# Strassen's seven block products for two of three output token tiles, on one Trainium2 core

## Chip, cores and metric

The kernel runs on one core of a Trainium2 chip. The metric is the device time of one execution in microseconds, as the median of the runs.

## The reference

Grouped-query attention (8 batches, 16 query heads, 4 key heads, 384 tokens, head size 64) is followed by a gated projection block with a spatial gate over the tokens:

```python
k = np.repeat(k, group, axis=1); v = np.repeat(v, group, axis=1)
scores = scale * np.matmul(q, k.transpose(0, 1, 3, 2))
attn = softmax(scores)                       # over the last axis
x = np.matmul(attn, v).transpose(0, 2, 1, 3).reshape(B, S, H * D)   # 8 x 384 x 1024
h = np.maximum(x @ w_in, 0.0)                # 1024 -> 1024
u, v = h[..., :512], h[..., 512:]
v_n = (v - mean(v)) / np.sqrt(var(v) + 1e-06)
v_s = np.einsum('ts,bsd->btd', w_spatial, v_n) + b_spatial[None, :, None]
out = (u * v_s) @ w_out                      # 512 -> 1024, float32
```

The last line is the output projection that the change is about: for each batch 384 x 512 times 512 x 1024.

## The kernel before

Everything is in float16 on TensorE (PE), with float32 sums in PSUM's eight banks. The 384 tokens of a batch are three tiles of 128. One batch of attention is 18 units (three query tiles, two head pairs, three key tiles); a unit's scores are two matmuls of 512 columns (`units`, L281), whose exponentials ACT writes as `aT` (L293). `weigh` (L301) multiplies them with V in twelve short matmuls, and DVE divides by the sum: a reciprocal (L315) and a product (L317) into `x16`. `x_send` (L341) has SP's queue transpose `x16` into `xt`.

The second half of the work is a stream of pieces, written as a generator, `gated` (L513), batch by batch:

- `v_part(b, st)`: eight matmuls of 512 columns (L357); DVE takes the relu out of PSUM into `vr` (L371). `measure` adds DVE's statistics (L383, L384) at the next `weigh`, or at once in the last batch.
- `u_part(b, m)`: eight matmuls of 384 columns (L438); ACT takes the relu (L449).
- `root` and `norm`: ACT makes the inverse root, DVE `nmr` (L396), and POOL writes the three normalized tiles `vn` (L401).
- `s_part(b, m)`: three matmuls of 384 columns with the spatial weights (L457); DVE adds the bias (`vs`, L469), and POOL multiplies with `uT` into `gT[:, m]` (L474). In the last batch's last m, DVE does the first token tile and POOL the others (L477).
- `o_part(b, tt, half)`: four matmuls of 512 columns, `gT` of 128 tokens against 512 columns of `w_out` (L495), summed in one bank. DVE copies it to `osb` (ACT for the second half of tile 1, L218), and after the second half SP's queue stores the tile (L510).

The output pieces of batch b - 1 are spread over batch b's stream: two after `v_part(b, 0)`, the others before each `s_part(b, m)`; in the last batch one after `v_part(7, 0)`, then one before each `s_part` and one after them. Batch 7's own come at the end.

The main loop (L773) goes in steps of three units. Each step issues six score matmuls, and between these and two groups of `weigh` it pours pieces of the stream in four portions, 0.2, 0.3, 0.1 and 0.4 of a share. The share is a sixth of a batch's planned matmul time:

```python
STEP = (NT * NK * C512 + NM * NK * C384 + NM * NT * C384 + 6 * NM * C512) / SETS
```

(17,496 / 6 = 2,916 ns; 15% less before unit 90). A piece counts at 216 ns for 512 columns and 162 for 384. What was poured too much or too little is carried over. What is left at the end of attention follows without pause. So the queues' order is fixed when the program is written: each engine takes its instructions in it.

PSUM banks are planned at the same time: `bank` (L79) takes the bank with the earliest planned end, and `reads` (L90) moves a planned clock of the reading engine on and sets that end:

```python
def reads(eng, ns, name=None):
    clock[eng] = max(clock[eng], clock[nc.tensor] + 200.0) + ns
    if name:
        done[taken.pop(name)] = clock[eng]
```

Only operations that call `reads` are on this planned clock.

The functions that the diff touches:

Of the kernel before, what the change touches and what calls it, by code (L numbers as in the profile page):

```python
# [9 lines left out]
FP32 = mybir.dt.float32  # L10
FP16 = mybir.dt.float16
I32 = mybir.dt.int32
AF = mybir.ActivationFunctionType
ALU = mybir.AluOpType
# [4 lines left out]
def kernel(  # L19
# [14 lines left out]
    nc = tc.nc  # L34
    P = 128
    B, HQ, S, D = q.shape
    HKV = k.shape[1]
    DM = moe_w_in.shape[0]
    DFF = moe_w_in.shape[1]
    DH = DFF // 2  # L40
    NT = S // P
    NK = DM // P
# [9 lines left out]
    order = ctx.enter_context(ExitStack())  # L52
    order.enter_context(tc.manual_schedule())

    cst = ctx.enter_context(tc.tile_pool(name="cst", bufs=1))
    ld = order.enter_context(tc.tile_pool(name="ld", bufs=2))
    att = order.enter_context(tc.tile_pool(name="att", bufs=2))
    moe = order.enter_context(tc.tile_pool(name="moe", bufs=2))
    small = order.enter_context(tc.tile_pool(name="small", bufs=4))
    ops = order.enter_context(tc.tile_pool(name="ops", bufs=3))  # L60
# [8 lines left out]
            name=nc.get_next_instruction_name(), act_func_set_id=set_id, ins=[], outs=[]  # L69
        )  # L70
    )
    pool, dve, act, sp = nc.gpsimd, nc.vector, nc.scalar, nc.sync
# [6 lines left out]
    def bank(shape, dtype, name):  # L79
        i = min(range(8), key=done.__getitem__)  # L80
        t = ps.tile(shape, dtype, name=name, tag=f"bank{i}")
        clock[nc.tensor] = max(clock[nc.tensor], done[i])
        done[i] = 1e12 + clock[nc.tensor]
        taken[name] = i
        return t

    def spend(ns):
        clock[nc.tensor] += ns
# [6 lines that stand above are left out]
    C512, C384, C128 = 216, 162, 56  # L95
# [59 lines left out]
    w_out16 = cst.tile([P, NM, DM], FP16, name="w_out16")  # L155
# [60 lines left out]
    def copy(eng, o, i, name):  # L216
        reads(eng, 600.0 if name.startswith("po") else 430.0, name)
        (act.copy if eng is act else dve.tensor_copy)(o, i)  # L218
# [45 lines left out]
    aTs, x16s, xts = {}, {}, {}  # L264
# [58 lines left out]
        measure()  # L323

    def new_xt(b):
        xts[b] = att.tile([P, NK, S], FP16, name=f"xt_{b}", tag="xt", bufs=3)

    def x_turn(b, qt, lo, hi, eng):
        if qt == 0 and lo == 0:
# [16 lines left out]
    v_r, v_n, mvs, uTs, gTs = {}, {}, {}, {}, {}  # L346
# [3 lines left out]
    def v_part(b, st, lo=0, hi=NK):  # L350
        if st == 0 and lo == 0:
            mvs[b] = small.tile([P, NT, 2], FP32, name=f"mv_{b}", tag="mv")
        if lo == 0:
            pvs[b, st] = bank([P, 512], FP32, f"pv_{b}_{st}")
        pv = pvs[b, st]
        for kt in range(lo, hi):
            nc.tensor.matmul(  # L357
                pv,
                xts[b][:, kt, st * P : (st + 1) * P],
                w_in16[:, kt, DH:DFF],  # L360
                start=(kt == 0),
                stop=(kt == NK - 1),
            )
            spend(C512)
            if kt < NK - 1:
                yield C512
        if hi < NK:
            return
        reads(dve, 610.0, f"pv_{b}_{st}")
        vr = moe.tile([P, DH], FP32, name=f"vr_{b}_{st}", tag="vr", bufs=6)  # L370
        dve.tensor_scalar(vr, pv, 0.0, None, op0=ALU.max)  # L371
        v_r[b, st] = vr
        unmeasured.append((b, st))
        if b == B - 1:
            measure()
        yield C512

    def measure():
        while unmeasured:
            b, st = unmeasured.pop()  # L380
            reads(dve, 800.0)
            stats = small.tile([P, 6], FP32, name=f"stats_{b}_{st}", tag="stats")
            dve.bn_stats(stats, v_r[b, st])  # L383
            dve.bn_aggr(mvs[b][:, st], stats)  # L384
# [8 lines left out]
    def norm(b):  # L393
        rstd = mvs[b, "rstd"]
        nmr = small.tile([P, NT], FP32, name=f"nmr_{b}", tag="nmr")
        dve.scalar_tensor_tensor(  # L396
            nmr, mvs[b][:, :, 0], -1.0, rstd, op0=ALU.mult, op1=ALU.mult
        )
        for st in range(NT):
            vn = moe.tile([P, DH], FP16, name=f"vn_{b}_{st}", tag="vn", bufs=6)  # L400
            (dve if b == 0 and st == 1 else pool).tensor_scalar(  # L401
                vn,
                v_r.pop((b, st)),
                rstd[:, st : st + 1],
                nmr[:, st : st + 1],
                op0=ALU.mult,
                op1=ALU.add,
            )
            v_n[b, st] = vn
# [67 lines left out]
                eng.tensor_tensor(gT[:, :, t], vs[:, :, t], uT[:, :, t], ALU.mult)  # L477
        yield C384

    osbs = {}  # L480

    def o_part(b, tt, half):
        last = b == B - 1
        if half == 0:
            osbs[b, tt] = ops.tile([P, DM], FP32, name=f"osb_{b}_{tt}", tag="osb")
        osb = osbs[b, tt]
        rows = out[b].rearrange("(p t) d -> p t d", t=NT)

        parts = [(half * 512, 512, act if half and (last or tt == 1) else dve, sp)]
        if last and tt == NT - 1 and half:  # L490
            parts = [(512, 384, dve, sp), (896, 128, act, act)]
        for c0, width, eng, queue in parts:
            po = bank([P, 512], FP32, f"po_{b}_{tt}_{c0}")
            for m in range(NM):
                nc.tensor.matmul(  # L495
                    po[:, 0:width],
                    gTs[b][:, m, tt * P : (tt + 1) * P],
                    w_out16[:, m, c0 : c0 + width],
                    start=(m == 0),
                    stop=(m == NM - 1),  # L500
                )
                spend(C512 * width / 512)
                if m < NM - 1:
                    yield C512 * width / 512
            cols = slice(c0, c0 + width)
            copy(eng, osb[:, cols], po[:, 0:width], f"po_{b}_{tt}_{c0}")
            if last:
                queue.dma_start(rows[:, tt, cols], osb[:, cols])
            elif half:
                sp.dma_start(rows[:, tt, :], osb)  # L510
            yield C512 * width / 512

    def gated():  # L513
        for b in range(B):
            u0 = b * UNITS
            behind = [(b - 1, tt, half) for tt in range(NT) for half in range(2)] if b else []
            if b == 0:
                for st in range(NT):
                    yield ("from", 6 * st + 7)
                    yield from v_part(b, st, 0, 4)  # L520
                    yield ("from", 6 * st + 10)
                    yield from v_part(b, st, 4, 8)
            else:
                yield ("from", u0 + 12)
                yield from v_part(b, 0)
                for _ in range(1 if b == B - 1 else 2):
                    yield from o_part(*behind.pop(0))
                yield ("from", u0 + 18)
                yield from v_part(b, 1)
                yield ("from", u0 + 24)  # L530
                yield from v_part(b, 2)
            for m in range(NM):
                i = 0
                for x in u_part(b, m):
                    yield x
                    i += 1
                    if (m, i) == (1, 6):
                        root(b)
                    if (m, i) == (2, 3):
                        norm(b)  # L540
                    if (b, m, i) == (B - 1, 2, 5):
                        judge()
            for m in range(NM):
                if (b, m) == (B - 1, 2):
                    count()
                if behind:
                    yield from o_part(*behind.pop(0))
                yield from s_part(b, m)
            if behind:
                yield from o_part(*behind.pop(0))  # L550
        for tt in range(NT):
            for half in range(2):
                yield from o_part(B - 1, tt, half)
# [39 lines left out]
    def at(n, f, *args):  # L593
        todo.setdefault(n, []).append((f, args))
# [92 lines left out]
    at(29, load_v, 2)  # L687
    at(31, load_q, 2, 1, sp, (1, 2))
    at(36, cast_v, 2, pool)
    for j, n in ((0, 34), (1, 36)):  # L690
        at(n, cast_q, 2, j, pool, (1, 2))
        at(n + 1, q_send, 2, j, 1, NT)
# [112 lines left out]
    with tc.If(counted != 0x43000000, preferred_fallthrough_block=False), ExitStack() as ctx:  # L805
        again = ctx.enter_context(tc.tile_pool(name="again", bufs=1))
        t = {
            n: again.tile([P, *w], I32 if n == "i32" else FP32, name=f"again_{n}")
            for n, w in (
                ("qg", (G * D,)), ("sc", (G, S)), ("p16", (16,)), ("row", (DH,)), ("kv", (16 * D,)),  # L810
                ("prod", (16 * D,)), ("one", (4,)), ("w", (4 * DM,)), ("f4", (4,)), ("acc", (DM,)),
                ("x", (DM,)), ("i32", (S,)),
            )
        }
# [224 lines left out]
```

## Time and profile before

| | |
|---|---|
| median of 3 runs | 240.33 us (239.26 to 242.33) |
| profiled execution | 239.11 us |
| span of its instructions | 237.1 us |
| PE matmuls busy | 230.1 us (97%), 2313 instructions |
| PE weight loads (PEld) | 123.7 us (52%) |
| DVE / ACT / POOL busy | 144.0 / 169.3 / 102.1 us |
| granted PE clock | 1.00 in every stage |
| output matmuls (L495) | 188 of 512 columns, 4 of 384, 4 of 128 |

The duration of a single matmul in the profile (380 ns for 512 columns) includes its way through the array; successive ones start closer together, so busy sums of PE do not show the rate. In the groups, the columns are: line, engine, operation, tile written and tiles read, shapes, count, then busy time and the mean of one in ns, then the idle time of the engine just before them and what ended it. The chain of waits is followed back from the last instruction; its lines are start, duration, and the engine and line. In the timeline the columns are start, duration, engine, line and operation.

### The profile page before, as it was taken

What the parts mean: (1) busy time and instruction counts of PE and PEld (TensorE: products, weight loads), DVE (VectorE), ACT (ScalarE), POOL (GpSimd) and SP (SyncE); (2) the same over time, 40 slices, a digit from 0 to 9 for tenths busy, and PEclk for the clock granted to TensorE, in tenths of its full rate; (3) what the DMA queues carried; (4) which work ended last, traced back from release to release, by engine and by line L of the source; (5) the groups of instructions that cost most, each with busy time, mean ns of one, the idle gap of its engine ahead of it and who ended that gap; (6) DMA issues with size and microseconds to landing.
All of it is one profiled execution on the core that took longest, in us unless ns stands there. A gap on an engine that the chain in (4) does not pass through costs nothing.

```text
span 237.1 us, 5939 instructions
## 1 busy us (share of the span) xinstructions
PE 230.1 (97%) x2313; PEld 123.7 (52%) x2313; DVE 144.0 (61%) x382; ACT 169.3 (71%) x349; POOL 102.1 (43%) x149
## 2 busy tenths in 40 slices
PE   7899999999999999999999999999999999999992
PEld 6555655545554546554564555554465455545541
DVE  2668774676456764566656576376645577377462
ACT  2899989968997869977797776985697776402211
POOL 3489583651566343274055700575031500550740
PEclk9999999999999999999999999999999999999999
DMA  6999999999999999989979899479902642340256
GB/s 168 282 319 316 272 145 165 199 292 223 308 227 210 244 374 177 243 240 294 181 230 234 235 211 287 85 250 182 254 3 60 114 174 56 46 177 0 91 212 233
DMA packets 67469, 47.48 MB, mean 200 GB/s; under 512 B 48336, under 2 KB 60416, under 8 KB 67440
## 3 DMA queue, kind: packets, MB, share of 16 engines
q1 hardware_dynamic: 62512, 39.86, 69.9%
q0 software_dynamic: 3952, 6.42, 12.0%
q10 hardware_dynamic: 976, 0.82, 1.2%
q8 instruction: 18, 0.29, 0.5%
q14 instruction: 11, 0.09, 0.1%
HBM read 25.95 MB, written 12.58 MB: 163 GB/s over the span
## 4 chain that ended last, share of the span: by engine, by line
PE 86%; DMA 6%; DVE 2%; SPq 1%; POOL 1%; issue 0%; ACTq 0%; ACT 0%
PE pu L438 17%; PE po L495 17%; PE pv L357 17%; PE sc L281 14%; PE av L301 13%; PE psp L457 6%; DMA q<-in_q_dram 4%; DMA qT<-q 2%; SPq L258 1%; PE qps L240 1%; POOL vn L401 1%; PE xps L334 1%; DVE x L317 1%; DVE qT L218 1%; DVE osb L218 1%; POOL q L206 0%
## 5 line engine op out<-in xcount | busy, mean ns | idle before, releaser
L293 ACT ACTIVATE aT<-sc 128x512 f16<-128x512 f32 x288 | 147.4, 621 | 30.9 <-PE sc L281 30.3
L301 PEld LDWEIGHTS <-aT 128*128 128x128 f16 x1152 | 47.0, 97 | 17.1 <-issue 1.9
L357 PE MATMUL pv<-w_in,xt 128*128 128x512 f16 x192 | 51.0, 380 | 0.1
L301 PE MATMUL av<-v,aT 128*128 128x65 f16 x1152 | 50.5, 193 | 0.0
L495 PE MATMUL po<-w_out,gT 128*128 128x512 f16 (+2 forms) x196 | 50.5, 375 | 0.0
L438 PE MATMUL pu<-xt,w_in 128*128 128x384 f16 x256 | 49.9, 327 | 0.0
L401 POOL TENSOR_SCALAR vn<-vr,rstd,nmr 128x512 f16<-128x512 f32 x23 | 17.6, 779 | 67.0 <-DVE nmr L396 45.6
L474 POOL TENSOR_TENSOR gT<-vs,uT 128x384 f16<-128x384 f32 x31 | 32.4, 1057 | 31.0 <-DVE r_all L315 16.9
L317 DVE TENSOR_TENSOR x<-av,r_all 128x256 f16<-128x256 f32 x96 | 40.8, 424 | 3.3
L281 PE MATMUL sc<-qT,kT 64*128 64x512 f16 x288 | 41.5, 380 | 0.5 <-DVE qT L218 0.2
L315 DVE RECIPROCAL r_all<-av 128x4 f32<-128x4 f32 x96 | 17.1, 179 | 40.5 <-PE av L301 40.1
L218 DVE COPY osb<-po 128x512 f32<-128x512 f32 (+1 forms) x39 | 26.6, 683 | 15.9 <-PE po L495 15.9
L438 PEld LDWEIGHTS <-w_in 128*128 128x128 f16 x256 | 22.1, 98 | 17.1 <-issue 5.5
L449 ACT ACTIVATE uT<-pu 128x384 f16<-128x384 f32 x32 | 15.8, 495 | 16.0 <-PE pu L438 15.8
L495 PEld LDWEIGHTS <-gT 128*128 128x128 f16 x196 | 17.3, 97 | 17.3 <-issue 3.2
L357 PEld LDWEIGHTS <-xt 128*128 128x128 f16 x192 | 15.8, 97 | 17.8 <-issue 5.5
L281 PEld LDWEIGHTS <-kT 64*128 64x128 f16 x288 | 10.9, 94 | 23.7 <-issue 12.3
L457 PE MATMUL psp<-wsT,vn 128*128 128x384 f16 x96 | 22.2, 327 | 0.0
L469 DVE TENSOR_TENSOR vs<-psp,bias_bc 128x384 f32<-128x384 f32 x32 | 17.6, 552 | 7.1 <-PE psp L457 6.9
L203 POOL CAST q<-q 128x768 f16<-128x768 f32 x22 | 17.6, 831 | 9.5 <-DMA q<-in_q_dram 4.5
L371 DVE TENSOR_SCALAR vr<-pv 128x512 f32<-128x512 f32 x24 | 16.4, 683 | 8.4 <-PE pv L357 8.3
L383 DVE BATCH_NORM_STATS2 stats<-vr 128x6 f32<-128x512 f32 x24 | 16.4, 685 | 0.1
(55 smaller groups left out, 101.9 us busy)
## 6 DMA issues: line engine op xcount, KB each, us to landing
out_dram<-osb SPq DMA_DIRECT2D x21, 512.0 KB, 3.2
q<-in_q_dram SPq DMA_DIRECT2D x10, 768.0 KB, 5.9
v_None<-in_v_dram SPq DMA_DIRECT2D x6, 384.0 KB, 5.7
w_in<-in_moe_w_in_dram POOLq DMA_DIRECT2D x4, 512.0 KB, 9.8
k_None<-in_k_dram SPq DMA_DIRECT2D x5, 384.0 KB, 3.7
q<-in_q_dram POOLq DMA_DIRECT2D x2, 768.0 KB, 7.6
out_dram<-osb SPq DMA_DIRECT2D x5, 256.0 KB, 3.1
w_out<-in_moe_w_out_dram POOLq DMA_DIRECT2D x2, 512.0 KB, 8.6
```

The source lines that it names most:

```text
L203: eng.tensor_copy(t16[:, :, :, hh, :], src[:, hh])
L218: (act.copy if eng is act else dve.tensor_copy)(o, i)
L281: nc.tensor.matmul(sc, kTs[b][rows, j, kt * P : (kt + 1) * P], qTs[b, j][rows, qt].rearrange("p (r i c) -> p i r c", r=G, i=G), start=True ...
L293: act.activation(a, sc, AF.Exp, scale=scale)
L301: nc.tensor.matmul(av[:, i * (D + 1) : (i + 1) * (D + 1)], aT[:, kt, hh, i * P : (i + 1) * P], v1[b % 2][:, 2 * j + hh, kt, 0 : D + 1], st ...
L317: dve.tensor_tensor(x16s[b][:, qt, c : c + 256].rearrange("p (i d) -> p i d", i=G), o[:, :, 0:D], r.to_broadcast([P, G, D]), ALU.mult,)
L357: nc.tensor.matmul(pv, xts[b][:, kt, st * P : (st + 1) * P], w_in16[:, kt, DH:DFF], start=(kt == 0), stop=(kt == NK - 1),)
L401: (dve if b == 0 and st == 1 else pool).tensor_scalar(vn, v_r.pop((b, st)), rstd[:, st : st + 1], nmr[:, st : st + 1], op0=ALU.mult, op1=A ...
L438: nc.tensor.matmul(pu[:, 0:S], w_in16[:, kt, m * P : (m + 1) * P], xts[b][:, kt, :], start=(kt == 0), stop=(kt == NK - 1),)
L457: nc.tensor.matmul(psp[:, 0:S], v_n[b, st][:, m * P : (m + 1) * P], wsT16[:, st, :], start=(st == 0), stop=(st == NT - 1),)
L474: pool.tensor_tensor(gT, vs, uT, ALU.mult)
L495: nc.tensor.matmul(po[:, 0:width], gTs[b][:, m, tt * P : (tt + 1) * P], w_out16[:, m, c0 : c0 + width], start=(m == 0), stop=(m == NM - 1),)
```

## The change

For batches 1 to 6 (`fast(b)`), token tiles 0 and 1 are taken as one product of two-by-two blocks: A has 128 tokens by 256 inner columns (rows of `gT`), W has 256 inner rows by 512 output columns. Seven products (`f_part(b, n)`, two matmuls each) take the place of eight block products (sixteen matmuls). Their left and right sides are blocks or sums of blocks:

- 1: A11 W11. 2: A12 W21. 3: S4 W22. 4: A22 T4. 5: S1 T1. 6: S2 T2. 7: S3 T3.
- S1 = A21 + A22, S2 = S1 - A11, S3 = A11 - A21, S4 = A12 - S2; they are `gS`, made by `g_combine(b)` on DVE (256 elements a partition each, float16).
- T1 to T4 are sums of blocks of `w_out`, made once by `w_combine` on DVE (1,024 elements a partition, float16) at units 42, 45, 48 and 51.

Product 1 comes at the end of batch b's stream, and ACT copies it to `part`. After `v_part(b + 1, 0)` come `g_combine(b)` and products 2 and 6; products 7 and 5 stand before `s_part(b + 1, 0)`, products 4 and 3 before `s_part(b + 1, 1)`, and tile 2's two pieces before the next two. In batch 7 products 4 and 3 are a place apart, and the last piece follows `s_part(7, 3)`. Each of products 2 to 7 is added on DVE straight from PSUM to a partial sum, product 5 twice. Tile 0 is stored after product 3, tile 1 after product 4. Batches 0 and 7 and all third tiles keep `o_part`. Batch 0's first four output matmul groups keep their places, written in the new form. Buffers of `xt` go from 3 to 2, of `vr` from 6 to 4, of `vn` from 6 to 3.

```diff
-        xts[b] = att.tile([P, NK, S], FP16, name=f"xt_{b}", tag="xt", bufs=3)
+        xts[b] = att.tile([P, NK, S], FP16, name=f"xt_{b}", tag="xt", bufs=2)
...
-        vr = moe.tile([P, DH], FP32, name=f"vr_{b}_{st}", tag="vr", bufs=6)
+        vr = moe.tile([P, DH], FP32, name=f"vr_{b}_{st}", tag="vr", bufs=4)
...
-            vn = moe.tile([P, DH], FP16, name=f"vn_{b}_{st}", tag="vn", bufs=6)
+            vn = moe.tile([P, DH], FP16, name=f"vn_{b}_{st}", tag="vn", bufs=3)
...
-    osbs = {}
+    osbs, halves16, partial = {}, {}, {}
+    w_out_t = cst.tile([P, 4, 2, 512], FP16, name="w_out_t")
+    def fast(b):
+        return 0 < b < B - 1
+    def w_combine(i):
+        b11, b12, b21, b22 = (w_out16[:, r : r + 2, c : c + 512] for r in (0, 2) for c in (0, 512))
+        t = [w_out_t[:, k] for k in range(4)]
+        x, y = ((b12, b11), (b22, t[0]), (b22, b12), (t[1], b21))[i]
+        dve.tensor_tensor(t[i], x, y, ALU.subtract)
+    def g_combine(b):
+        t = halves16[b] = moe.tile([P, 4, 2, P], FP16, name=f"gS_{b}", tag="gS", bufs=1)
+        a11, a12, a21, a22 = (
+            gTs[b][:, r : r + 2, c : c + P] for c in (0, P) for r in (0, 2)
+        )
+        dve.tensor_tensor(t[:, 0], a21, a22, ALU.add)
+        dve.tensor_tensor(t[:, 1], t[:, 0], a11, ALU.subtract)
+        dve.tensor_tensor(t[:, 2], a11, a21, ALU.subtract)
+        dve.tensor_tensor(t[:, 3], a12, t[:, 1], ALU.subtract)
+    def f_part(b, n):
+        if n == 2:
+            for tt in range(2):
+                osbs[b, tt] = ops.tile([P, DM], FP32, name=f"osb_{b}_{tt}", tag="osb")
+        if n == 1:
+            partial[b] = moe.tile([P, 3, 512], FP32, name=f"part_{b}", tag="part", bufs=1)
...
+        name = f"pf_{b}_{n}"
+        po = bank([P, 512], FP32, name)
+        for m in range(2):
+            nc.tensor.matmul(po, left(m), right(m), start=(m == 0), stop=(m == 1))
+            spend(C512)
+            if m == 0:
+                yield C512
+        s1, s2, s3 = (partial[b][:, k] for k in range(3))
+        s4 = s1
+        lo, hi = slice(0, 512), slice(512, 1024)
+        if n == 1:
+            copy(act, s1, po, name)
+        else:
+            o, x, y, op = {
+                2: (osbs[b, 0][:, lo], po, s1, ALU.add),
+                6: (s2, po, s1, ALU.add),
+                7: (s3, po, s2, ALU.add),
+                5: (s4, po, s2, ALU.add),
+                4: (osbs[b, 1][:, lo], s3, po, ALU.subtract),
+                3: (osbs[b, 0][:, hi], po, s4, ALU.add),
+            }[n]
+            if n == 5:
+                reads(dve, 690.0)
+                dve.tensor_tensor(osbs[b, 1][:, hi], po, s3, ALU.add)
+            reads(dve, 690.0, name)
+            dve.tensor_tensor(o, x, y, op)
...
     def gated():
         for b in range(B):
             u0 = b * UNITS
-            behind = [(b - 1, tt, half) for tt in range(NT) for half in range(2)] if b else []
+            if not b:
+                behind = [[] for _ in range(5)]
+            elif fast(b - 1):
+                order = ((2, 6), (7, 5), (4, 3), ((2, 0),), ((2, 1),), ())
+                if b == B - 1:
+                    order = ((2, 6), (7, 5), (4,), (3,), ((2, 0),), ((2, 1),))
...
                 yield from v_part(b, 0)
-                for _ in range(1 if b == B - 1 else 2):
-                    yield from o_part(*behind.pop(0))
+                if fast(b - 1):
+                    g_combine(b - 1)
+                yield from next_behind()
...
+            yield from next_behind()
+            if fast(b):
+                yield from f_part(b, 1)
...
+    for i in range(4):
+        at(42 + 3 * i, w_combine, i)
```

More of the change, by code (lines that the diff above doesn't have):

```diff
@@ new lines, in f_part @@
+    def f_part(b, n):
[4 more added lines that the diff above has]
+            partial[b] = moe.tile([P, 3, 512], FP32, name=f"part_{b}", tag="part", bufs=1)
+        g, s, w, t = gTs[b], halves16.get(b), w_out16, w_out_t
+        left, right = {
+            1: (lambda m: g[:, m, 0:P], lambda m: w[:, m, 0:512]),
+            2: (lambda m: g[:, 2 + m, 0:P], lambda m: w[:, 2 + m, 0:512]),
+            3: (lambda m: s[:, 3, m], lambda m: w[:, 2 + m, 512:1024]),
+            4: (lambda m: g[:, 2 + m, P : 2 * P], lambda m: t[:, 3, m]),
+            5: (lambda m: s[:, 0, m], lambda m: t[:, 0, m]),
+            6: (lambda m: s[:, 1, m], lambda m: t[:, 1, m]),
+            7: (lambda m: s[:, 2, m], lambda m: t[:, 2, m]),
+        }[n]
[19 more added lines that the diff above has]
+                3: (osbs[b, 0][:, hi], po, s4, ALU.add),
+            }[n]
+            if n == 5:
[3 more added lines that the diff above has]
+            dve.tensor_tensor(o, x, y, op)
+        for tt, end in ((0, 3), (1, 4)):
+            if n == end:
+                sp.dma_start(out[b].rearrange("(p t) d -> p t d", t=NT)[:, tt, :], osbs[b, tt])
+        yield C512
@@ L515, in gated, with next_behind @@
             u0 = b * UNITS
-            behind = [(b - 1, tt, half) for tt in range(NT) for half in range(2)] if b else []
+            if not b:
[4 more added lines that the diff above has]
+                    order = ((2, 6), (7, 5), (4,), (3,), ((2, 0),), ((2, 1),))
+                behind = [
+                    [f_part(b - 1, n) if isinstance(n, int) else o_part(b - 1, *n) for n in ns] for ns in order
+                ]
+            else:
+                behind = [[o_part(b - 1, tt, half)] for tt in range(NT) for half in range(2)]
+                if b < B - 1:
+                    behind = [behind[0] + behind[1], *behind[2:], []]
+            def next_behind():
+                for x in behind.pop(0):
+                    yield from x
             if b == 0:
@@ L545, in gated @@
                     count()
-                if behind:
-                    yield from o_part(*behind.pop(0))
+                yield from next_behind()
                 yield from s_part(b, m)
-            if behind:
-                yield from o_part(*behind.pop(0))
+            yield from next_behind()
+            if fast(b):
+                yield from f_part(b, 1)
         for tt in range(NT):
```

## The prediction, before the changed kernel was run

> **What bounds the kernel.** I read the page's head first (which engine is full, and at what clock), then busy time by stage, then the chain of waits for the end, then the groups for prices, and last the timeline around the places that the change touches.
>
> ```profile
> PE 230.1 (97%) x2313; PEld 123.7 (52%) x2313; DVE 144.0 (61%) x382; ACT 169.3 (71%) x349; POOL 102.1 (43%) x149
> PEclk9999999999999999999999999999999999999999
> 160.10:187.20 27.10, 27.10 (x276) 14.16 (x273) 16.52 (x44) 20.85 (x44) 8.37 (x10) 1.00 0.59 126
> ```
>
> The third line is one batch (PE, PEld, DVE, ACT, POOL, then clock, DMA). A full PE row may hide pipelining, so I count starts instead. 24 back-to-back output matmuls take 5.19 us in the chain below: 0.216 each. With 384 columns three take 0.49: 0.162 each; six score matmuls with their switch of tile shape take 0.85, twelve attention ones 0.37. One batch is then 24 x 0.216 (gate) + 32 x 0.162 + 12 x 0.162 + 24 x 0.216 (output) + 6 x 0.85 + 12 x 0.37 = 27.0 us. The stage took 27.04 from 160.18 to 187.22. So TensorE has no hole there: a matmul saved is 0.216 us saved, and a wait in PE's queue is lost in full. DVE is busy 16.5 of 27.
>
> ```profile
> 226.68 5.19 PE po L495 x24
> 231.90 1.21 DVE osb L218 x2
> ```
>
> The end hangs on PE's own work too, and then on two copies.
>
> **Prices.** Groups (busy, mean ns):
>
> ```profile
> L317 DVE TENSOR_TENSOR x<-av,r_all 128x256 f16<-128x256 f32 x96 | 40.8, 424 | 3.3
> L218 DVE COPY osb<-po 128x512 f32<-128x512 f32 x38 | 26.1, 686 | 15.9 <-PE po L495 15.9
> L469 DVE TENSOR_TENSOR vs<-psp,bias_bc 128x384 f32<-128x384 f32 x32 | 17.6, 552 | 7.1 <-PE psp L457 6.9
> L218 DVE COPY qT<-qps 128x512 f16<-128x512 f16 x12 | 5.1, 422 | 2.4 <-PE qps L240 2.3
> L396 DVE SCALAR_TENSOR_TENSOR nmr<-mv,rstd 128x3 f32<-128x3 f32 x8 | 1.3, 160 | 4.4 <-ACT rstd L390 4.4
> ```
>
> An f32 operation has about 0.155 us fixed (nmr) and one element per cycle: x and vs differ by 128 elements and 0.128 us. A recombining operation (512 f32, PSUM and SBUF to SBUF) is vs plus 128 elements, 0.69, and lets the next unrelated one start after 0.63. A sum of token blocks (256 elements, all f16, SBUF) is not in the trace. From above x bounds it, 0.42; from below, the fixed part with two elements per cycle, 0.155 + 0.133 = 0.29. That f16 to f16 goes at two per cycle is seen in qT: 512 elements in 0.42 where the f32 copy takes 0.69. I take 0.29, since its operands are qT's kind, and keep 0.42 for the range. The Trainium skill ("VectorE: DVE Perf Modes", The perf-mode tier table) says that a two-tensor operation on 16-bit SBUF data reaches twice the rate, and no more than that; by it the sum stays at 0.29 and a faster sum is excluded. No row here has a two-tensor f16 operation, so the trace neither confirms nor refutes it.
>
> **1. Removed: matmuls.** Two tiles of a batch took 16 matmuls and take 14. 6 x 2 x 0.216 = -2.59 us. This is all that the change can gain.
>
> **2. DVE gets more.** Per batch three copies go (ACT keeps one as before); seven recombinations (product 5 has two) and four sums come: -3 x 0.686 + 7 x 0.69 + 4 x 0.29 = +3.9 us, so 20.4 of 27 busy. That alone costs nothing; what counts is who waits in its queue.
>
> **3. Product 6 waits for its sums.** The four sums are queued on DVE behind the relu of `v_part(b+1, 0)`; product 6 needs the second. On PE only product 2 (0.43) and whatever attention work the pacing puts there stand between. The timeline has the place twice:
>
> ```profile
> 107.43 0.38 PE L357 MATMUL pv<-w_in,xt 128*128 128x512 f16 x1
> 107.65 1.03 PE L495 MATMUL po<-w_out,gT 128*128 128x512 f16 x4
> 107.85 0.42 DVE L317 TENSOR_TENSOR x<-av,r_all 128x256 f16<-128x256 f32 x1
> 108.19 0.68 DVE L371 TENSOR_SCALAR vr<-pv 128x512 f32<-128x512 f32 x1
> 108.79 0.68 DVE L218 COPY osb<-po 128x512 f32<-128x512 f32 x1
> 211.57 1.03 PE L495 MATMUL po<-w_out,gT 128*128 128x512 f16 x4
> 212.50 0.69 DVE L383 BATCH_NORM_STATS2 stats<-vr 128x6 f32<-128x512 f32 x1
> 213.33 0.67 DVE L218 COPY osb<-po 128x512 f32<-128x512 f32 x1
> ```
>
> Let T be the start of PE's next instruction after the last v matmul. DVE's relu starts 0.20 later (211.57, 211.77), the next operation 0.61 after that. First sum 0.29, 0.04 to a dependent one (relu to statistics: 212.46 to 212.50), second sum 0.29, then 0.15 to the matmul (0.06 for a semaphore, as gT at 227.93 to the weight load at 227.99, and 0.1 for the load). Chain: 0.20 + 0.61 + 0.29 + 0.04 + 0.29 + 0.15 = 1.58.
>
> Where it falls comes from the pacing: ahead of product 2 of batch b the new order has 2b - 4 fewer matmuls than the old one has ahead of its first output tile there (two more for b = 1), while the attention groups stand where they stood. Batch 2: as at 107.65, relu late behind x; first sum 108.79, product 6 at 109.56 where PE is ready at 108.08: 1.48. Batch 5: same place, relu 0.12 late: 1.27. Batches 1 and 4: a score group (0.85) lies between, cover 1.28: 0.42 and 0.30. Batch 3: score group and twelve attention matmuls, cover 1.65: 0. Batch 6, in the tail: batch 7's statistics stand ahead of the sums. First sum at 213.33, second ends 213.95, product 6 at 214.10, PE ready at 212.00: 2.10. Sum **+5.57**. With 0.42 for a sum it would be 7.2.
>
> **4. Banks come back late.** Product 2's recombination stands behind all four sums, which the bank planner's clock (line 90) does not count; its bank is given to the next but one tile. In batches 1 and 4 DVE frees it 2.5 to 2.6 us after T and PE asks at 2.0 to 2.1: **+1.0** for both. In the loop over m, products 7, 5, 4, 3 bring five operations of 0.63 among vs and attention. Batch 4, from the end of product 7 at 0: DVE has 7 until 0.83, 5 until 2.09, vs until 2.59, an attention pair until 3.14, product 4 until 3.83. PE meanwhile does product 5 (0.43), a psp (0.49), twelve attention matmuls (0.37), products 4 and 3 (0.86), two thirds of a psp (0.33) and five score matmuls (0.62), and asks for product 4's bank at 3.1 and for product 3's after that: 0.78 + 0.25 = 1.0. The same count gives 0.4, 0.6 and 0.8 in batches 1 to 3, and nothing in 5, where attention is over. **+2.8**. From below this is 0: where the planner's choice falls otherwise, a free bank is at hand.
>
> **5. The tail.** With no attention between, DVE has in the last loop, from 0.63 us on, 5.75 us of work up to the last vs (five recombinations for products 7, 5, 4, 3, 3.15, four vs of 0.50, one copy of 0.60); gT of m = 3 follows: 0.63 + 5.75 + 0.04 + 0.44 = 6.86. PE has 5.40 of work up to batch 7's first tile and wants it at the fourth matmul, 6.05: 0.81 + 0.15 = **+0.95**. From below 0; before, only the weight loader waited there (0.29 us at 227.99).
>
> **6. Taken as nothing.** The four weight sums (1,024 elements, 0.69 each, 1.22 at most) come near 55 to 68 us, where DVE is busy 12.1 of 21 us, with room for them; uncovered they cost their 2.8 us. Buffers: xt of batch b is needed when the last readers of b - 2 are done: x_send of batch 6 was issued at 159.4, the readers of batch 4's ended at 151.4. vr and vn are read out a whole batch earlier than their reuse. Without this cover SP's queue would hold the q and k loads behind x_send. Output stores are as many, with the same bytes, now after products 3 and 4. ACT's copy moves from tile 1 to product 1: one for one.
>
> **Sum.** -2.59 + 5.57 + 1.0 + 2.8 + 0.95 = +7.7. The profiled execution took 239.11 us (span 237.1 and 2.0 around it), so 246.8. The median of the runs shown is 240.33, 1.2 above that execution: what is likely to be read lies at 246.8 or a little above, +2.7% against the median.
>
> **The rivals.**
> - *Only the sums are waited for* (0.27). The banks are found free, as before, where no wait for a bank shows in the steady stages; the order of the planner speaks against it. 239.1 - 2.6 + 5.6 = 242.1.
> - *The waits are covered, not slower* (0.09). The place is product 6: if the scheduler puts at least 1.6 us of PE work between the last v matmul and it, the 5.57 are gone, and so is what follows. Then 239.11 - 2.59 = 236.5. For it: DVE idles 39% of the span and ended almost none of PE's idle time. Against: the queues keep program order, and batch 3 alone has that cover. It decides from a chain shorter than 0.43.
> - *DVE becomes the bound* (0.12). The sums take 0.42 (+1.6 in step 3, +1.2 in step 4), weight sums are uncovered (+1.4): 251.
> - *The clock drops* (0.04). If each of the three waits over 1 us were followed by half clock for as long as it lasted, 1.5 + 1.3 + 2.1 = 4.9 us more: 251.7. The trace has 1.00 in every stage, in the first 10 us too, where PE is busy 8.0. The Trainium skill ("TensorE: Matmul & The Clock Gate", A second HAM failure mode) reports such throttling where PE idles briefly between groups in a cycle of PSUM banks; this trace has no idling to try it on.
> - That two matmuls a batch are not saved is excluded by the code; the remainder (0.03) is mishaps.
>
> **How the numbers follow.** My forecast, the whole sum, has 0.45. Range 241.0 to 251.0: the lower end takes steps 4 and 5 as nothing and some of step 3 covered, the upper one is DVE as the bound; outside lie the covered case and half of what is left. Two per cent, about what a measurement of this kernel can tell from no change, is 235.5 to 245.1. Slower by more: 0.41 of the forecast, 0.04 of the first rival, 0.12, 0.04: 0.61. Faster by more than 2% would need twice the saved matmuls: 0.02. The rest, 0.37, is within.
>
> **What would show it.** Right: 14 matmuls for two tiles; PE or its loader idle ahead of product 6 with DVE's sums as what ended it, least in batch 3, longest in batch 6; DVE busy near 170 us; score matmuls that end later than 0.75 us after their start in the loop over m. Wrong: stages of batches 4 to 6 at 26.6 us, without holes (covered), or sums of 0.42 and more; and, if DVE is late only at product 6, step 4.

## The result, and the profile after

The changed kernel takes 249.39 us (median of 4 runs, 248.27 to 249.71) against 239.91 us for the kernel before (4 runs): a ratio of 1.0398, 95% interval 1.0358 to 1.0437. The profiled execution took 249.56 us with a span of 247.8, against 239.11 and 237.1.

The engines' busy time, from the head of the page after:

```profile
PE 231.1 (93%) x2301; PEld 122.4 (49%) x2301; DVE 165.9 (67%) x434; ACT 169.9 (69%) x349; POOL 103.3 (42%) x149
PEclk9999999999999999999999999999999999999999
```

There are 12 matmuls fewer (2301 for 2313) and 52 DVE operations more, 22 us of DVE work. PE's busy sum has not fallen: a matmul's record lasts 0.38 us where the next could start after 0.216, so about 0.16 us of each wait counts as busy. Its share has, from 97 to 93%. The clock stayed where it was. Who ended PE's waits, from the list of waits after (total, times, longest); none of these was in the list of before:

```profile
PE pf L525 <- DVE gS L501: 4.7, 5, 1.8
...
PE po L566 <- POOL gT L474: 0.5, 1, 0.5
PE pf L525 <- POOL gT L474: 0.4, 1, 0.4
PE pv L357 <- DVE osb L547: 0.4, 1, 0.4
PE av L301 <- DVE osb L547: 0.4, 1, 0.4
PE av L301 <- DVE part L547: 0.4, 1, 0.4
```

The list gives only the time in which no matmul was under way, and puts a wait under the last releaser. To have all of it, I took PE's timeline of both executions and, for each group, the distance to the next group's start less what the same group takes without a wait (0.216 per 512 columns, 0.162 per 384, 0.366 per twelve attention matmuls, 0.855 per six score matmuls). By place, in us:

| place | predicted | measured after |
|---|---|---|
| product 6 waits for its sums, batches 1 to 6 | 0.42, 1.48, 0, 0.30, 1.27, 2.10 = 5.57 | 0.21, 1.36, 0.49, 0.39, 1.17, 1.96 = 5.58 |
| product 2's bank, batches 1 and 4 | 1.0 | 0.57 + 0.57 = 1.1 |
| banks in the loop over m, batches 1 to 4 | 0.4, 0.6, 0.8, 1.0 = 2.8 | 0.56, 0.68, 0.76, 1.29 = 3.3 |
| product 1 of batch 6 waits for gT | nothing | 0.57 |
| batch 7's first tile waits for gT | 0.95 | 0.70 |
| sum | 10.3 | 11.3 |

Less 2.6 for the matmuls that is +8.7 of the +10.45 between the two profiled executions. Another 0.89 lies ahead of anything that the change issues: the scores of step 42 start at 55.67 in place of 54.78 us. In other executions, which share this part of the program, they start between 54.2 and 56.5, so this is no effect of the change. The rest is in pieces under 0.12 us.

Three places in the timeline after (start, duration, engine, line, operation; here and below, lines between those shown are left out). First product 6 of batch 2, the place that the prediction showed at 107.65 us:

```profile
109.91 0.59 PE L525 MATMUL pf<-w_out,gT 128*128 128x512 f16 x2
110.45 0.68 DVE L371 TENSOR_SCALAR vr<-pv 128x512 f32<-128x512 f32 x1
111.05 0.28 DVE L500 TENSOR_TENSOR gS<-gT 128x256 f16<-128x256 f16 x1
111.36 0.29 DVE L501 TENSOR_TENSOR gS<-gS,gT 128x256 f16<-128x256 f16 x1
111.71 0.60 PE L525 MATMUL pf<-w_out_t,gS 128*128 128x512 f16 x2 [1.21 <-DVE gS L501]
```

Product 2 starts at 109.91 and could be followed at 110.34; the relu, the first and the second sum come after one another, and product 6 starts 0.06 us after the second ends. Then the tail, where batch 7's statistics stand ahead of the sums:

```profile
220.05 0.59 PE L525 MATMUL pf<-w_out,gT 128*128 128x512 f16 x2
220.97 0.69 DVE L383 BATCH_NORM_STATS2 stats<-vr 128x6 f32<-128x512 f32 x1
221.80 0.26 DVE L500 TENSOR_TENSOR gS<-gT 128x256 f16<-128x256 f16 x1
222.44 0.60 PE L525 MATMUL pf<-w_out_t,gS 128*128 128x512 f16 x2 [1.80 <-DVE gS L501]
```

Third, the loop over m with batch 4's products:

```profile
186.56 0.55 DVE L469 TENSOR_TENSOR vs<-psp,bias_bc 128x384 f32<-128x384 f32 x1
186.61 0.39 PE L281 MATMUL sc<-qT,kT 64*128 64x512 f16 x1
187.16 0.39 PE L281 MATMUL sc<-qT,kT 64*128 64x512 f16 x2 [0.17 <-DVE vs L469]
187.23 0.42 DVE L317 TENSOR_TENSOR x<-av,r_all 128x256 f16<-128x256 f32 x1
187.57 0.68 DVE L547 TENSOR_TENSOR osb<-part,pf 128x512 f32<-128x512 f32 x1
187.71 0.39 PE L281 MATMUL sc<-qT,kT 64*128 64x512 f16 x2 [0.16 <-DVE x L317]
188.30 0.37 PE L281 MATMUL sc<-qT,kT 64*128 64x512 f16 x1 [0.20 <-DVE osb L547]
188.60 0.10 PEld L457 LDWEIGHTS <-vn 128*128 128x128 f16 x1 [0.78 <-issue]
```

Six score matmuls, otherwise done in 0.75 us, are pulled apart to 2.0 (186.61 until the next weight load at 188.60): each pair waits for a bank that DVE frees in its own order, first a bias addition (`vs`), then an attention pair (`x`), then product 4's recombination.

### The profile page after: what moved, and what is told of

It reads as the page before. It is cut to its first block, busy times and chain, and to the rows that moved or that the text cites. A ratio compares the mean times of both kernels' runs of the same rounds, so it can differ in the third digit from the quotient of the medians.

```text
span 247.8 us, 5953 instructions
## 1 busy us (share of the span) xinstructions
PE 231.1 (93%) x2301; PEld 122.4 (49%) x2301; DVE 165.9 (67%) x434; ACT 169.9 (69%) x349; POOL 103.3 (42%) x149
## 5 line engine op out<-in xcount | busy, mean ns | idle before, releaser
L401 POOL TENSOR_SCALAR vn<-vr,rstd,nmr 128x512 f16<-128x512 f32 x23 | 18.1, 797 | 68.4 <-DVE nmr L396 47.3
L281 PE MATMUL sc<-qT,kT 64*128 64x512 f16 x288 | 43.5, 380 | 1.6 <-DVE x L317 0.3
L566 PE MATMUL po<-w_out,gT 128*128 128x512 f16 (+2 forms) x100 | 25.5, 371 | 0.6 <-POOL gT L474 0.5
L457 PE MATMUL psp<-wsT,vn 128*128 128x384 f16 x96 | 21.7, 326 | 0.0
L218 DVE COPY osb<-po 128x512 f32<-128x512 f32 (+1 forms) x21 | 14.2, 681 | 7.0 <-PE po L566 6.9
L525 PE MATMUL pf<-w_out_t,gS 128*128 128x512 f16 x36 | 10.1, 381 | 5.0 <-DVE gS L501 4.7
```

The source lines that it names most:

```text
L281: nc.tensor.matmul(sc, kTs[b][rows, j, kt * P : (kt + 1) * P], qTs[b, j][rows, qt].rearrange("p (r i c) -> p i r c", r=G, i=G), start=True ...
L401: (dve if b == 0 and st == 1 else pool).tensor_scalar(vn, v_r.pop((b, st)), rstd[:, st : st + 1], nmr[:, st : st + 1], op0=ALU.mult, op1=A ...
L457: nc.tensor.matmul(psp[:, 0:S], v_n[b, st][:, m * P : (m + 1) * P], wsT16[:, st, :], start=(st == 0), stop=(st == NT - 1),)
L566: nc.tensor.matmul(po[:, 0:width], gTs[b][:, m, tt * P : (tt + 1) * P], w_out16[:, m, c0 : c0 + width], start=(m == 0), stop=(m == NM - 1),)
```

## The experiments

Theory A: PE loses what its queue waits for, and this hangs on where DVE's new work stands in DVE's queue. Theory B: DVE's 22 us of added work are paid for wherever they stand. Theory C: the side parts (fewer buffers, weight sums) cost the time. Every kernel was compared with runs of the kernel before on the same chip, and ratios go by these.

**What the saved matmuls are worth.** The kernel before, with the first of four matmuls left out in twelve output pieces:

```diff
+            skip = 0 < b < B - 1 and tt < 2 and half == 0
-            for m in range(NM):
+            for m in range(1 if skip else 0, NM):
```

> The kernel before with 12 matmuls left out: the first of the four in the first half of tiles 0 and 1 of batches 1 to 6, so these halves sum three products in place of four. Nothing else changes. It prices the removed matmuls alone. By the prediction's first step: 12 x 0.216 = 2.6 us less, 237.3 us against a before of 239.9. If saved matmuls are worth less than their start-to-start distance (they would only uncover another wait), 238.5 to 239.9.

Measured: 237.12 us, ratio 0.9914 (0.9894 to 0.9934), so 2.1 us less, 1.6 to 2.5 by the interval. PE's timeline shows no new wait. The gain is there, a little under its 2.6.

**The side parts alone.** The kernel before with the smaller buffers (three places, shortened here) and the weight sums:

```diff
-tag="xt", bufs=3 / tag="vr", bufs=6 / tag="vn", bufs=6
+tag="xt", bufs=2 / tag="vr", bufs=4 / tag="vn", bufs=3
+    for i in range(4):
+        at(42 + 3 * i, w_combine, i)
```

> The kernel before with only the side parts of the change: xt in 2, vr in 4, vn in 3 buffers, and the four weight sums on DVE, whose results nothing reads. Theories A and B: within 0.5 us of before for the buffers, up to 1 us for the weight sums: 239 to 240. Theory C (buffers and weight sums cost the time): 245 or more.

Measured: 239.58 against 239.75 us, ratio 0.9993 (0.9968 to 1.0019). Theory C falls.

**Without the sums.**

```diff
-                if fast(b - 1):
-                    g_combine(b - 1)
...
-            6: (lambda m: s[:, 1, m], lambda m: t[:, 1, m]),
+            6: (lambda m: g[:, m, 0:P], lambda m: t[:, 1, m]),
```

(and likewise for products 3, 5 and 7)

> The four sums of token blocks are left out altogether; products 3, 5, 6 and 7 read blocks of gT in their place, so the products are other ones, with the same matmuls and recombinations. Theory A: no wait ahead of product 6 and none for product 2's bank: 249.4 - 5.6 - 1.1 = 242.7 us, and the loop over m keeps its 3.3. Theory B: the sums are 6.8 of the 22 us that came to DVE, so of the 12 us between the saved matmuls and the result 3.7 go: 245.7. Theory C: 249.

Measured: 242.69 us, ratio 1.0167 (1.0145 to 1.0189). This is A's number; B's 245.7 is out. In PE's timeline the waits ahead of product 6 and for product 2's bank are gone, and the loop over m keeps 3.3 us.

**Sums ahead of the relu.**

```diff
-                yield from v_part(b, 0)
-                if fast(b - 1):
-                    g_combine(b - 1)
+                for i, x in enumerate(v_part(b, 0)):
+                    yield x
+                    if i == 5 and fast(b - 1):
+                        g_combine(b - 1)
```

> Only the place of the four sums moves: DVE gets them after the sixth v matmul, so ahead of the relu instead of behind it (and, in batch 7, ahead of the statistics). Theory A (PE loses what its queue waits for, by place: 5.6 us ahead of product 6, 1.1 for product 2's bank, 3.3 for banks in the loop over m, 1.3 for gT in the tail): the waits ahead of product 6 go to 0.5 us or less in all, product 2's bank comes about 0.6 earlier, the rest stays: about 243.5 to 244.5 us. Theory B (DVE's 22 us of added work are paid for wherever they stand): no change, 249 us. Theory C (fewer buffers and the weight sums cost the time): no change either.

Measured: 247.85 us, ratio 1.0375 (1.0356 to 1.0394): 4 us more than A said, and by the intervals no clear gain over the changed kernel. By its time alone this is the "no change" of B and C; the trace shows another reason. In the tail product 6's wait did fall, from 1.96 to 0.38, and over all batches from 5.6 to 2.7. But elsewhere the relu now came late. DVE, POOL and PE from this kernel's timeline:

```profile
136.57 1.67 POOL L203 CAST q<-q 128x768 f16<-128x768 f32 x2
136.80 0.75 DVE L500 TENSOR_TENSOR gS<-gT 128x256 f16<-128x256 f16 x1 [0.22 <-POOL gT L474]
137.58 0.79 DVE L501 TENSOR_TENSOR gS<-gS,gT 128x256 f16<-128x256 f16 x1
138.18 0.88 POOL L191 CAST v<-v_None 128x768 f16<-128x768 f32 x1
138.30 0.90 DVE L502 TENSOR_TENSOR gS<-gT 128x256 f16<-128x256 f16 x1
139.33 0.68 DVE L371 TENSOR_SCALAR vr<-pv 128x512 f32<-128x512 f32 x1
140.06 0.52 PE L301 MATMUL av<-v,aT 128*128 128x65 f16 x12 [1.57 <-DVE vr L371]
```

Sums that take 0.28 elsewhere take 0.75 to 0.90 beside POOL's casts. The four hold DVE from 136.80 to 139.40, and PE waits for the bank that the relu frees: 1.75 us by its starts. In batch 4 product 6 itself waits 1.11 us, behind the same four and the relu. So the place does matter, but I had the wrong object: it is not product 6 alone that must not wait for the sums, but anything queued behind them on DVE.

**Product 6 later.**

```diff
-                order = ((2, 6), (7, 5), (4, 3), ((2, 0),), ((2, 1),), ())
+                order = ((2,), (6,), (7, 5), (4, 3), ((2, 0),), ((2, 1),), ())
...
                 yield from v_part(b, 1)
+                if fast(b - 1):
+                    yield from next_behind()
```

> Only product 6 moves, from behind product 2 to behind v_part(b+1, 1); the sums stay behind the relu of v_part(b+1, 0). Theory A: PE has 1.7 us of matmuls and often attention between the relu and product 6, so its 5.6 us of waits go; product 2's recombination still stands behind the sums (1 to 1.5 us of bank waits, one or two more where a POOL cast slows the sums): 243.5 to 245. Theory B: 249. If what hurts at this place is DVE held up by the sums, whoever waits for it, rather than product 6 itself: 246 to 248.

Measured: 247.14 us, ratio 1.0293 (1.0257 to 1.0328): the third reading. Ahead of product 6 only 0.2 us of waits is left, but the next to be served by DVE now waits, product 2's bank:

```profile
111.83 0.60 PE L357 MATMUL pv<-w_in,xt 128*128 128x512 f16 x2
114.17 0.64 PE L301 MATMUL av<-v,aT 128*128 128x65 f16 x12 [1.74 <-DVE osb L547]
114.62 1.90 PE L357 MATMUL pv<-w_in,xt 128*128 128x512 f16 x4
```

The four v matmuls behind this wait start 0.43 us apart, where 0.216 is usual: the trace has a granted clock of 0.50 from 114.44 to 117.85 us. The page's row of clock tenths shows it as one 7:

```profile
PEclk9999999999999999997999999999999999999999
```

This execution took 249.50 us, the other three of this kernel 246.15 to 247.23.

**Sums behind product 2.** The same, with the call of `g_combine` moved one line down, behind product 2:

```diff
                 yield from v_part(b, 0)
-                if fast(b - 1):
-                    g_combine(b - 1)
                 yield from next_behind()
+                if fast(b - 1):
+                    g_combine(b - 1)
```

> As the kernel in which only product 6 moved behind v_part(b+1, 1), but the four sums are given to DVE behind product 2's recombination in place of ahead of it. Nothing else moves. If its remaining loss at this place is product 2's bank, held because its recombination stands behind the sums (4 to 4.5 us of waits in that kernel): 243 to 244 us. If any DVE work at this place is paid for: 247 as there. The bank waits in the loop over m (2.9 us) and gT waits in the tail (1.3) stay in both.

Measured: 245.44 us, ratio 1.0230 (1.0194 to 1.0266), between the two. The waits for product 2's bank are gone (4 us of starts in the kernel before this one). But in batch 2 the sums meet POOL's casts, hold the attention pair behind them, and PE waits 1.0 us there and 1.2 soon after; and product 6 waits for its sums again, 0.4 us in batch 3 and 0.9 in batch 6. DVE and POOL in batch 2's stretch:

```profile
110.10 0.28 DVE L500 TENSOR_TENSOR gS<-gT 128x256 f16<-128x256 f16 x1
110.14 1.76 POOL L203 CAST q<-q 128x768 f16<-128x768 f32 x2 [2.56 <-DMA q<-in_q_dram]
110.42 0.80 DVE L501 TENSOR_TENSOR gS<-gS,gT 128x256 f16<-128x256 f16 x1
111.14 0.90 DVE L502 TENSOR_TENSOR gS<-gT 128x256 f16<-128x256 f16 x1
111.97 0.90 DVE L503 TENSOR_TENSOR gS<-gT,gS 128x256 f16<-128x256 f16 x1
```

**Only the burst split.** Products 7 and 5 move between the u parts, the rest stays:

```diff
-                order = ((2, 6), (7, 5), (4, 3), ((2, 0),), ((2, 1),), ())
+                order = ((2, 6), (7,), (5,), (), (4, 3), ((2, 0),), ((2, 1),), ())
...
                         judge()
+                if m in (0, 2) and b and fast(b - 1):
+                    yield from next_behind()
```

> Only products 7 and 5 move, from before s_part(b+1, 0) to after the first and the third u part. Theory A: the bank waits in the loop over m (3.3 us in the changed kernel) and part of the gT waits in the tail (1.3) go: 245 to 246 us; the waits ahead of product 6 stay at 5 to 6. Theory B: 249.

Measured: 244.51 us, ratio 1.0240 (1.0184 to 1.0297), 4 to 5 us less than the changed kernel, about where A had it. In the loop over m 0.2 us of waits are left of 3.3, and those for gT are gone; product 6's stay at 5.8.

**A first spread order.** Product 6 behind `v_part(b+1, 1)`, products 7, 5, 4 and 3 behind the four u parts:

```diff
-                order = ((2, 6), (7, 5), (4, 3), ((2, 0),), ((2, 1),), ())
+                order = ((2,), (6,), (7,), (5,), (4,), (3,), ((2, 0),), ((2, 1),), (), (), ())
```

> The same arithmetic in another order: product 6 stands after v_part(b+1, 1), products 7, 5, 4, 3 after the four u parts, one each (in batch 7 products 4 and 3 stay in the loop over m); the sums stay where they are. DVE has the same work as in the changed kernel. Theory A: v_part's 1.7 us of matmuls cover the sums, the recombinations no longer come in a burst with the bias additions; PE's waits fall to 1 us or so, and the saved matmuls show: 238.5 us, range 237.3 to 240.5. Theory B: 249 us as before. In between, 241 to 246: the place explains only a part.

Measured: 245.92 us, ratio 1.0291 (1.0275 to 1.0307); A's 238.5 was missed by 7. Two new waits took the place of the old. With no products between them, the s parts came too close for POOL's 1.06 us per gT, and product 1 waited for gT in five batches (0.36 to 0.92 us). And the sums still stood ahead of product 2's recombination: in batch 4 the attention matmuls waited 1.36 us for its bank.

**Everything spread.** So the order must give POOL its time as well, and must not put four sums in a row:

```diff
-                order = ((2, 6), (7, 5), (4, 3), ((2, 0),), ((2, 1),), ())
+                order = ((2,), (6,), (7,), (), (5,), (), (4,), (3,), ((2, 0),), ((2, 1),), ())
...
+        reads(dve, 300.0)
+        dve.tensor_tensor(t[:, i], x, y, op)
...
-                yield from v_part(b, 1)
+                for i, x in enumerate(v_part(b, 1)):
+                    yield x
+                    if i in (1, 5) and fast(b - 1):
+                        g_combine(b - 1, i // 4)
...
```

(`g_combine(b, i)` now makes one sum; the other two come likewise within `v_part(b, 2)`, and product 6 follows)

> All waits found so far are taken away by order alone, with the same arithmetic: the four sums go to DVE one at a time, two within v_part(b+1, 1) and two within v_part(b+1, 2), on the planned clock at 300 ns each; product 6 follows v_part(b+1, 2); products 7 and 5 stand between the u parts, products 4 and 3 and tile 2's pieces before the four s parts, so that the s parts stay apart and gT has its time. Theory A (waits by place; the saved matmuls are worth 1.9 us as the kernel with twelve fewer showed): waits of 1 to 2 us in all stay, 238 to 239.5 us against 239.0 before. Theory B (DVE's added work is paid for wherever it stands): 246 us or more, as the first spread order. A third theory, that sums slowed by POOL's casts (0.5 to 0.9 us in place of 0.28 where they meet) are what counts: 241 to 243, since the casts fall into v_part(b+1, 1) too.

Measured: 238.25 us, ratio 0.9945 (0.9919 to 0.9970). DVE does the same work as in the changed kernel (166.1 us busy, there 165.9), on the same data, and 11 us are gone. B falls, and so does the third theory with its 241 to 243. Sums still meet POOL's casts (three take 0.56 to 0.82), but one at a time, and nothing on PE waits for that. What is left is 0.9 us ahead of batch 7's first tile, and 0.4 in a score group behind a weight sum that took 1.20 us. Besides the order, this kernel differs in that the sums are on the bank planner's clock (`reads`); no run has the one without the other, so how much of the 11 us is due to banks chosen otherwise is not shown.

**The tail too.**

```diff
-                    order = ((2,), (6,), (), (7,), (), (5,), (4,), (3,), ((2, 0),), (), ((2, 1),))
+                    order = ((2,), (6,), (7,), (), (5,), (), (4,), (3,), ((2, 0),), (), ((2, 1),))
...
-        parts = [(half * 512, 512, act if half and (last or tt == 1) else dve, sp)]
+        parts = [(half * 512, 512, act if b == B - 2 or half and (last or tt == 1) else dve, sp)]
```

> The kernel with everything spread, and two edits for its tail, where it still waits 0.9 us for gT: in batch 7 products 7 and 5 stand after the first and the third u part as in the other batches, so that DVE is free when the first bias addition comes, and ACT, idle there, makes both copies of batch 6's third tile. Theory A: POOL's first gT starts about 0.6 us earlier and the wait falls to 0.3 us or less: 237.6 us against 238.2 for the kernel with everything spread. If POOL's three gT of 1.06 us in a row are what is waited for, whenever they start: no change.

Measured: 237.27 us, ratio 0.9921 (0.9894 to 0.9949), the lowest of all orders tried, and as fast as the kernel with twelve matmuls left out (0.9914). By its interval it is not clear of the kernel with everything spread; in the trace the wait ahead of batch 7's first tile fell from 0.9 to 0.2 us. Its page, engines and chain:

```profile
PE 228.7 (97%) x2301; PEld 123.1 (52%) x2301; DVE 164.2 (70%) x432; ACT 170.8 (73%) x351; POOL 103.5 (44%) x149
PE 91%; DVE 4%; POOL 1%; DMA 1%; issue 1%; SPq 0%; DVEq 0%
```

PE is full again, with DVE at 70%, and the chain of waits is PE's own once more; in the changed kernel it could be followed back over the last 62 us only, and went from DVE to PE and back there.

## Why the prediction came out

**Step 1, removed matmuls: right in kind, a little large.** Worth 2.1 us (1.6 to 2.5) by the kernel with twelve fewer, 2.6 in the sum.

**Step 2, DVE's load: right.** The busy time grew by 22 us where the working had 26; operation by operation it is 27, since busy time counts overlapping ones once. A sum took 0.28 where I had 0.29, a recombination 0.68 where I had 0.69. On the question that the Trainium skill answered ("VectorE: DVE Perf Modes", The perf-mode tier table: twice the rate for two 16-bit operands in SBUF) the trace agrees: 0.28 us for 256 elements, and not the 0.42 of the f32 row. That this load by itself costs nothing is shown by the last kernel.

**Step 3, product 6: right in size, and each place but one.** 5.58 for 5.57, but that the two agree so closely is luck. Batch 3, taken as covered, waited 0.49, because its first two sums took 0.47 and 0.79 us beside POOL's casts, which the step did not consider; the other five batches waited 0.48 less than forecast, batch 1 only half of its 0.42, and batch 4's 0.39 too has a slowed sum in it (0.58). The step said that product 6 waits; the runs showed that taking away half of this wait (sums ahead of the relu) is worth 0.5 us by the ratios, and nearly all of it (product 6 later) 2.5, because what comes next in DVE's queue then waits.

**Step 4, banks: right, 0.6 short.** 4.4 for 3.8. The kernel without sums took the 1.1 for product 2's bank away, the one with the burst split nearly all of the 3.3 in the loop over m.

**Step 5, the tail: part of it wrong.** Batch 7's first tile waited 0.70 where I had 0.95. But step 4's "nothing in 5, where attention is over" was too short a look: banks were free, but the same burst of recombinations delayed batch 6's bias additions and with them POOL's gT, and product 1 waited for the second of its two blocks. In the kernel with only the burst split this wait is gone. In the changed kernel:

```profile
216.99 3.18 POOL L474 TENSOR_TENSOR gT<-vs,uT 128x384 f16<-128x384 f32 x3 [0.67 <-DVE vs L469]
217.30 0.38 PE L525 MATMUL pf<-w_out,gT 128*128 128x512 f16 x1
218.09 0.39 PE L525 MATMUL pf<-w_out,gT 128*128 128x512 f16 x1 [0.42 <-POOL gT L474]
```

**Step 6, taken as nothing: right.** Ratio 0.9993 for the side parts; the weight sums took 0.66 to 0.93 us each in the changed kernel without a wait of note beside them. It is not quite nothing: in the last kernel one of 0.99 us stands ahead of an attention pair, and a score group waits 0.3 us.

**The sum.** +7.7 was forecast, +9.5 came by the medians (8.6 to 10.5 by the interval). 1.0 of the difference is in the table of waits, 0.5 in the price of a matmul.

**The rivals.** "Only the sums are waited for" (242.1) fell: the banks' part is in the trace. "Covered" needed the order to be another, and with another order it is what happens. "DVE becomes the bound" was near in time (251) for the wrong reason: the same DVE work fits behind a full PE. "The clock drops" did not come in the changed kernel: 1.00 in the tenths, 0.998 in the mean, with waits of up to 1.96 us in PE's queue, and product 6's longest in the batch where PE had no attention to do. So the second failure mode that the Trainium skill describes ("TensorE: Matmul & The Clock Gate", A second HAM failure mode) did not appear in it.

This rival is not out for waits of this size, though. In the kernel with product 6 later, 1.74 us without a matmul were followed by 3.41 us at a clock of 0.50; with matmuls 0.43 us apart that costs 1.7 us, an estimate from these figures. The kernel with twelve matmuls fewer has such a stretch at 0.50 too, from 12.98 to 16.39 us, ahead of the first matmul left out. Stretches of like length without a matmul, 1.80 us in the changed kernel's tail and 1.57 with the sums ahead of the relu, were not followed by one. What decides is not shown.

## What to carry to other kernels

Where PE is full and the queues' order is fixed, as here, trading matmuls for vector work paid only when every operation of that work had a place where nothing behind it in its queue was due: count who stands behind it, not only who reads it. Taking away a wait that the profile names can move it to the next in the same queue, as it did for the sums; it need not, as the split burst shows, whose waits went almost in full. The gain over the kernel before showed only when the sums, the recombinations and the third engine (here POOL's gT) all had their places. That is the difference between +4.0% and -0.8% with the same arithmetic.

## What the hardware showed besides

Sums of two f16 tiles in SBUF on DVE depend on what POOL does. In the changed kernel 21 of 24 took 0.26 to 0.29 us, and the three that started within a POOL cast took 0.47, 0.58 and 0.79; in the kernel with the sums ahead of the relu five did, at 0.72 to 0.90. Each of these eight ended 0.14 to 0.15 us after a cast ended, whether 0.32 or 0.76 us of that cast was left when it started. POOL's casts beside them took 0.82 to 0.89 us, against at most 0.87 in the kernel before. It goes the other way too: a cast of 768 elements that starts within a sum takes longer than its usual 0.83 us, 0.94 in the kernel with product 6 later (behind a sum of gT), and 1.28 in the kernel with everything spread (started 0.59 us ahead of the end of a weight sum). The Trainium skill states it ("SBUF — State Buffer", Who interferes with whom): a DVE instruction with two SBUF inputs contends with a POOL instruction that reads SBUF, since its second input comes through a read interface that they share, and the sharing is an exclusive lock. The trace agrees: whichever starts second waits out most of what is left of the other, and the recombinations, with one input in PSUM, kept 0.66 to 0.69. That the one causes the other rests on these overlaps; no run here moved the casts.
